# Two KB of scratch for POOL's transfers, the identity in the constants' tile, rooms fixed by name

## The chip, the cores and the metric

One core of one Trainium2 chip. The time is that of one execution on the device, in microseconds (us). The engines are TensorE (PE, its weight loads PEld), VectorE (DVE), ScalarE (ACT), GpSimd (POOL) and SyncE (SP); SP and POOL issue nearly all transfers.

## The reference

Attention over pooled keys and values, then a gated feed-forward network, all in float32:

```python
# q, k, v: (8, 8, 576, 64); keys and values are means over 8 neighbours, so 72 of each
scores = q @ k_p.transpose(0, 1, 3, 2) / 8
attn = exp(scores - max) / (sum + 1e-09)
x = (attn @ v_p).transpose(0, 2, 1, 3).reshape(4608, 512)
out = (sigmoid(x @ w_gate) * (x @ w_val)) @ w_out        # 512 -> 1536 -> 512
```

## The kernel before

The 4608 rows of x are worked on in nine blocks of 512. Block 0 goes first, alone, by a hand-written word list (`ORDER`, carried out by `first_pass`). The other eight go in four rounds of two. A round makes the gate and value products of two blocks as a 2x2 scheme with seven products in place of eight (`product`, tiles `chain`), then the products with `w_out` in the same scheme (`second_sums`, tiles `acc`). Each float32 operand is split in a high and a low part, and each product is made of three products of parts. In between stands the attention of the blocks to come (`attention`), as tasks cut into steps.

Weights are read once as 64-bit words, converted, split, kept in the chip's main memory (`kept...`) and read again in each round: `parts` for gate and value through six rooms, `oparts` for `w_out` through three, issued two units ahead in `second_sums`.

In blocks 4 to 8 the transposes that attention needs are not TensorE's. `turned` has DVE transpose blocks of 32x32 (tile `turn`), then POOL issues 4 to 8 transfers to main memory (tile `turned`) for each call and one back (to `pt` or `pr`). POOL also writes the weights' parts to main memory in round 1 (`reload` with `fresh`). These are the only transfers that POOL issues, and a scratch in the first bytes of each partition serves them: 1024 bytes, an argument of `bacc.Bacc`.

Nothing is issued while the functions run. `Book` takes each call as a numbered unit (a unit can hold several matmuls), and the loop at the end issues the units in the order of the list `LATER`; so the sequence on each engine and queue is fixed by hand. Waits follow from which tile an instruction reads or writes.

Rooms: the pool `rawp` has three rooms in rotation for loads of q, k and v (tile `raw`), `two` has two in rotation for `y` (also `o`) and two for `m`. Rotation gives the next tile a room, and its first writer waits for the readers of the tile before in that room.

Constants: `cst` (128 partitions, 133 words) holds an identity, masks and one number. SP loads it with `nc.sync.dma_start(cst, const)`, as its fifth load. DVE casts the identity to `identr` (type F32R) for the transposes of `r3`. `spare` is a small tile on which POOL's fill and an ACT exponential run at the start.

Of the kernel before, what the change touches and what calls it, by code (L numbers as in the profile page):

```python
# [11 lines left out]
F32 = mybir.dt.float32  # L12
# [7 lines left out]
P = 128  # L20
# [90 lines left out]

LATER = """
# [217 lines left out]
def attention_then_ffn(ctx: ExitStack, tc: tile.TileContext, qT, kT, vm, vr, vn, sums8, wgv, wo, const, out, outT):  # L330
# [34 lines left out]
    def split(h, l, x):  # L365

        nc.scalar.copy(h, x)
        nc.vector.tensor_tensor(out=l, in0=x, in1=h.bitcast(F32), op=ALU.subtract)

    kept = {
        (kind, p, g): dram.tile([P, 2, 2 * HALF], F32R, name=f"kept{kind}{p}{g}")
# [1204 lines left out]
```

## Time and profile before

| | |
|---|---|
| median of 3 runs | 906.82 us (906.38 to 906.93) |
| profiled execution, time | 906.25 us |
| its span, first to last instruction | 904.5 us |
| PE busy | 893.6 us (99%) |
| DVE busy | 657.4 us (73%) |
| ACT busy | 497.1 us (55%) |
| POOL busy | 199.4 us (22%) |
| transfers of POOL's queue (q0) | 15040 packets, 32.79 MB, 10.6% of 16 engines' span |
| transfers of SP's queue (q1) | 85040 packets, 203.84 MB, 66.7% |

The span is the time that the rows below speak of; the execution is 1.75 us longer than it. A matmul's length is modelled and overlaps the next one's, so the mean of one is longer than what it adds. "issue" as the end of an idle time says that nothing in the profile released the instruction. Nearly all rows carry the line 317, which is that of the helper that records calls; the names of the tiles tell them apart.

### The profile page before, as it was taken

How to read it: one execution, taken by the hardware profiler on the slowest of the kernel's cores; microseconds unless marked ns; L12 is line 12 of the kernel's file. 1: busy time of each engine (PE TensorE's matmuls, PEld its weight loads, DVE VectorE, ACT ScalarE, POOL GpSimd, SP SyncE). 2: the span in 40 equal slices, each digit the busy share in tenths (PEclk: the TensorE clock that was granted, in tenths of full speed). 3: DMA queues.
4: the chain of work that ended last, by engine and by line, in shares of the span. 5: the costliest groups of instructions: out<-in, count | busy, mean ns of one | idle time of the engine just before them, and what ended most of it. 6: DMA issues, size and time to landing. Idle time of an engine off the chain costs nothing.

```text
span 904.5 us, 12612 instructions
## 1 busy us (share of the span) xinstructions
PE 893.6 (99%) x4162; PEld 735.1 (81%) x4162; DVE 657.4 (73%) x1039; ACT 497.1 (55%) x1071; POOL 199.4 (22%) x369
## 2 busy tenths in 40 slices
PE   7999999999999999999999999999999999999998
PEld 6788778888888888888888888888888888888886
DVE  7989788889899998757678796356589552224863
ACT  5888887587856475445365554334355542224352
POOL 2412101011164235443343104132213000000000
PEclk9999999999999999999999999999999999999999
DMA  9899888889999888787987787686747775746644
GB/s 342 302 332 349 289 331 303 299 280 330 329 328 313 278 288 287 234 304 260 302 273 245 243 279 260 225 269 198 256 127 249 247 251 201 227 169 205 195 167 141
DMA packets 100289, 237.56 MB, mean 263 GB/s; under 512 B 13856, under 2 KB 34720, under 8 KB 98688
## 3 DMA queue, kind: packets, MB, share of 16 engines
q1 hardware_dynamic: 85040, 203.84, 66.7%
q0 software_dynamic: 15040, 32.79, 10.6%
q8 instruction: 33, 0.54, 0.2%
q14 instruction: 32, 0.26, 0.1%
q10 hardware_dynamic: 144, 0.13, 0.0%
HBM read 176.02 MB, written 60.69 MB: 262 GB/s over the span
## 4 chain that ended last, share of the span: by engine, by line
PE 90%; DVE 4%; DMA 3%; ACT 2%; issue 1%; SPq 0%; DVEq 0%; ACTq 0%
PE chain L317 55%; PE acc L317 27%; PE av L317 4%; PE sc L317 3%; DVE early L317 1%; DMA raw<-in_wgv 1%; DMA raw_o<-in_wo 1%; PE tp L317 1%; DMA raw<-in_vr 1%; DMA h<-in_kT 0%; ACT e L317 0%; DVE s L317 0%; DVE hs L317 0%; DVE h L317 0%; ACT hs L317 0%
## 5 line engine op out<-in xcount | busy, mean ns | idle before, releaser
L317 PE MATMUL chain<-xo,parts 128*128 128x512 f32 x2316 | 543.7, 392 | 0.0
L317 PEld LDWEIGHTS chain<-xo,parts 128*128 128x128 f32 x2316 | 430.7, 188 | 92.5 <-issue 1.0
L317 PE MATMUL acc<-hs,oparts 128*128 128x512 f32 x1008 | 237.3, 391 | 0.3 <-issue 0.2
L317 PEld LDWEIGHTS acc<-hs,oparts 128*128 128x128 f32 x1008 | 188.0, 188 | 40.9 <-issue 1.2
L317 POOL DMA_DIRECT2D turned<-turn x240 | 131.7, 551 | 214.8 <-DVE turn L317 185.2
L317 DVE TENSOR_TENSOR y<-chain,sV 128x512 f32<-128x512 f32 x46 | 31.1, 686 | 69.3 <-PE chain L317 59.0
L317 DVE TENSOR_TENSOR hs<-h,hs 128x1024 fp32r<-128x1024 f32 x52 | 63.0, 1217 | 11.6 <-ACT hs L317 11.4
L317 ACT CAST hs<-h 128x1024 fp32r<-128x1024 f32 x52 | 54.4, 1050 | 30.0 <-PE acc L317 23.1
L317 ACT COPY chain<-chain 128x512 f32<-128x512 f32 x46 | 26.4, 576 | 57.0 <-PE chain L317 47.3
L317 DVE TENSOR_TENSOR y<-chain,sG 128x512 f32<-128x512 f32 x46 | 31.2, 682 | 34.0 <-PE chain L317 23.4
L317 ACT CAST hs<-s 128x1024 fp32r<-128x1024 f32 x36 | 37.5, 1051 | 28.4 <-PE acc L317 13.0
L317 ACT COPY sG<-chain 128x512 f32<-128x512 f32 x46 | 26.7, 586 | 46.5 <-PE chain L317 44.8
L317 DVE TENSOR_TENSOR hs<-s,hs 128x1024 fp32r<-128x1024 f32 x36 | 43.8, 1219 | 11.2 <-ACT hs L317 10.9
L317 ACT COPY sV<-chain 128x512 f32<-128x512 f32 x46 | 26.7, 585 | 38.8 <-PE chain L317 36.1
L317 DVE SCALAR_TENSOR_TENSOR h<-gate,chain 128x512 f32<-128x512 f32 x46 | 30.6, 677 | 21.8 <-PE chain L317 21.7
L317 ACT ACTIVATE gate<-chain 128x512 f32<-128x512 f32 x46 | 26.9, 594 | 34.2 <-PE chain L317 31.7
L317 PE MATMUL sc<-kbd,raw 128*128 128x144 f32 (+1 forms) x262 | 41.2, 296 | 0.1
L317 PEld LDWEIGHTS sc<-kbd,raw 128*128 128x128 f32 (+1 forms) x262 | 33.6, 176 | 7.9 <-issue 2.8
L317 ACT ACTIVATE gate<-y 128x512 f32<-128x512 f32 x46 | 28.9, 633 | 19.1 <-DVE y L317 19.0
L317 PE MATMUL acc<-oparts,hs 128*128 128x512 f32 x144 | 38.7, 402 | 0.2 <-ACT oparts L317 0.2
L317 DVE TENSOR_REDUCE m<-sc 128x4 f32<-128x288 f32 x48 | 21.7, 452 | 18.2 <-PE sc L317 17.7
L317 DVE SCALAR_TENSOR_TENSOR h<-gate,y 128x512 f32<-128x512 f32 x46 | 31.0, 683 | 0.3
(211 smaller groups left out, 1073.8 us busy)
## 6 DMA issues: line engine op xcount, KB each, us to landing
oparts<-keptS SPq DMA_DIRECT2D x48, 512.0 KB, 4.4
oparts<-keptO SPq DMA_DIRECT2D x72, 256.0 KB, 4.2
raw<-in_wgv SPq DMA_DIRECT2D x12, 1024.0 KB, 8.5
out<-o SPq DMA_DIRECT2D x35, 256.0 KB, 3.6
raw<-in_kT SPq DMA_DIRECT2D x28, 288.0 KB, 5.0
raw<-in_qT SPq DMA_DIRECT2D x29, 256.0 KB, 4.7
raw<-in_vm SPq DMA_DIRECT2D x24, 256.0 KB, 5.6
raw_o<-in_wo SPq DMA_DIRECT2D x12, 512.0 KB, 8.1
```

The lines of the kernel that those rows point to most:

```text
L317: return self._book.take(lambda: f(*args, **named))
```

## The change

Six edits:

- The scratch is 2048 bytes.
- `cst` is a tile of type F32R, 136 words; `cst` and `identr` are two views of it. The tile `identr` and DVE's cast are gone.
- The load of the constants is POOL's, with both sides as F32R.
- `spare` takes its room from the tag `rz`.
- The three rotating pools become one-room pools with tags that carry a number; strings (`RAWS`, `YS`, `MS`) give the number for each tile in the order in which the tiles are asked for.
- `LATER` is written anew for one unit less.

```diff
+RAWS = (
+    "21012001220111021201020120200212010202122010021021020121012010110021011220110"
+)
...
-6 5 4 7 0 11 3 2 21 8 25 27 19 28 14 18 23 31 22 20 9 26 13 35 17 36 33 1 10 40 45 76 39 37 12 48 47 52 16 55 32 66 38
...
-    cpool, work, two = sb("cpool"), sb("work"), sb("two", 2)
-    rawp, wpool, opool = sb("rawp", 3), sb("wpool"), sb("opool")
+    cpool, work, two = sb("cpool"), sb("work"), sb("two")
+    rawp, wpool, opool = sb("rawp"), sb("wpool"), sb("opool")
...
-    cst = cpool.tile([P, P + 16], F32, name="cst")[:, :P + 5]
+    constr = cpool.tile([P, P + 8], F32R, name="cst")[:, :P + 5]
+    cst, identr = constr.bitcast(F32), constr[:, :P]
...
-    identr = cpool.tile([P, P], F32R, name="identr")
-    spare = cpool.tile([P, 8], F32, name="spare")
+    spare = work.tile([P, LINE], F32, name="spare", tag="rz")[:, :8]
...
+    raws, ys, ms = iter(RAWS), iter(YS), iter(MS)
+
+    def raw_tile():
+        return rawp.tile([P, S], F32, name="raw", tag=f"raw{next(raws)}")
+
+    def y_tile(name):
+        return two.tile([P, BT], F32, name=name, tag=f"y{next(ys)}")
+
+    def m_tile():
+        return two.tile([P, LINE], F32, name="m", tag=f"m{next(ms)}")
...
-        return fill(rawp.tile([P, S], F32, name="raw"), *what)
+        return fill(raw_tile(), *what)
...
-        gate = two.tile([P, BT], F32, name="y", tag="y")
+        gate = y_tile("y")
...
-    nc.sync.dma_start(cst, const)
-    nc.vector.tensor_copy(identr, ident)
+    nc.gpsimd.dma_start(constr, const.bitcast(F32R))
...
-    nc = bacc.Bacc("TRN2", target_bir_lowering=False, num_devices=1, dynamic_dma_scratch_size=1024)
+    nc = bacc.Bacc("TRN2", target_bir_lowering=False, num_devices=1, dynamic_dma_scratch_size=2048)
```

## Rows read from the trace of the kernel before

**Rows 1.** Windows: length, busy us of PE, PEld, DVE, ACT, POOL, clock, transfers' share, GB/s.

```profile
0.00:28.00 28.00, 23.32 (x120) 18.38 (x121) 22.08 (x50) 17.09 (x38) 8.27 (x27) 1.00 0.94 343
28.00:248.00 220.00, 218.24 (x1073) 179.31 (x1072) 193.60 (x350) 175.38 (x480) 35.38 (x60) 1.00 0.89 313
248.00:707.00 459.00, 458.89 (x2128) 379.51 (x2127) 346.61 (x533) 232.12 (x449) 155.48 (x283) 1.00 0.80 261
707.00:904.50 197.50, 193.13 (x847) 157.94 (x845) 95.15 (x108) 72.53 (x107) 0.26 (x1) 1.00 0.58 198
```

**Rows 2.** TensorE's waits, whole span: who waited for whom, us, times, longest.

```profile
PE idle L317 <- POOL kbd L318: 1.7, 1, 1.7
...
PE tp L317 <- ACT y L317: 0.7, 1, 0.7
...
PE av L317 <- DVE pl L317: 0.5, 1, 0.5
...
PE vr L317 <- DMA xs<-in_vn: 0.2, 1, 0.2
```

**Rows 3.** TensorE's waits after 248 us.

```profile
PE acc L317 <- issue: 0.2, 1, 0.2
```

**Rows 4.** The chain that ended last, first 32 us: start, us, what.

```profile
2.12 4.28 DMA h<-in_kT
...
7.54 0.13 DVE identr L317
...
20.43 0.62 PE tp L317 x4
```

**Rows 5.** Timeline of the start: start, us, engine, line, operation, tiles, shape, count, idle.

```profile
2.59 0.43 SPq L317 DMA_DIRECT2D cst<-in_const  x1
2.96 0.20 POOL L318 MEMSET vfull<- 128x128 f32 x1
...
6.42 0.75 DVE L317 TENSOR_REDUCE early<-h 128x72 f32<-128x576 f32 x1 [1.19 <-DMA h<-in_kT]
...
16.04 1.04 POOL L317 TENSOR_SCALAR w<-w 128x1024 f32<-128x1024 f32 x1 [12.87 <-ACT w L317]
```

**Rows 6.** The page's costliest groups, two of TensorE.

```profile
L317 PE MATMUL chain<-xo,parts 128*128 128x512 f32 x2316 | 543.7, 392 | 0.0
...
L317 PE MATMUL acc<-hs,oparts 128*128 128x512 f32 x1008 | 237.3, 391 | 0.3 <-issue 0.2
```

**Rows 7.** The tile cst: first reader (ns, first and last start); its load's landing.

```profile
L317 PE MATMUL tp<-cst,early x36: 270/273/328, 14.7 to 146.6; 128*128 128x128 f32 x36
...
DMA to landing us min/median/max: 4.0/4.0/4.0
```

**Rows 8.** The tiles turned: who waited for their transfers (us, times); landing.

```profile
  POOL pt L317: 12.8, 3
...
  DVE turn L317: 5.0, 3
...
DMA to landing us min/median/max: 1.7/3.9/7.1
```

**Rows 9.** POOL's timeline, one burst.

```profile
276.24 3.95 POOL L317 DMA_DIRECT2D turned<-turn  x7 [3.43 <-DVE turn L317]
281.51 0.55 POOL L317 DMA_DIRECT2D turned<-turn  x1 [1.31 <-issue]
```

**Rows 10.** That burst's first transfer alone.

```profile
DMA to landing us min/median/max: 5.0/5.0/5.0
```

**Rows 11.** POOL's waits that end without a releaser, ahead of turned.

```profile
POOL turned L317 <- issue: 12.2, 13, 2.6
```

**Rows 12.** POOL's timeline, another burst.

```profile
247.43 0.53 POOL L317 DMA_DIRECT2D keptG2C<-parts  x1 [0.27 <-DVE vrc L317]
...
254.99 1.12 POOL L317 DMA_DIRECT2D turned<-turn  x2 [1.91 <-DMA keptG2C<-parts]
```

**Rows 13.** The page's transfers: count, KB each, median us to landing.

```profile
oparts<-keptS SPq DMA_DIRECT2D x48, 512.0 KB, 4.4
```

More of the change, by code (lines that the diff above doesn't have):

```diff
@@ L109 @@
 """
-LATER = """
[155 rows of a table removed]
+RAWS = (
+    "21012001220111021201020120200212010202122010021021020121012010110021011220110"
+)
+YS = (
+    "1001010110100110101010100001100100110101101010101010010110010101010110100110101001011000111010100110"
+    "10101001100101011011000110010101"
+)
+MS = (
+    "010101010101010101010101010101010101010101010101"
+)
+LATER = """
[150 rows of a table added]
 """
@@ L741, in attention @@
                 scv = sc.rearrange("p i (h k) -> p (i h) k", h=2)
-                m = two.tile([P, LINE], F32, name="m")[:, :QT]
+                m = m_tile()[:, :QT]
                 nc.vector.reduce_max(out=m, in_=scv, axis=AX.X, negate=j in BIASED)
@@ L896, in product @@
         if m in (3, 7):
-            y = two.tile([P, BT], F32, name="y", tag="y")
+            y = y_tile("y")
             nc.vector.tensor_tensor(out=y, in0=t, in1=seen[kind, {3: 6, 7: 5}[m]], op=ALU.add)
@@ L1077, in result @@
             else:
-                t = two.tile([P, BT], F32, name="o", tag="y")
+                t = y_tile("o")
             r, a = (half * 2 + c) * P, (2 * n - 2 + side) * BT
@@ L1202, in first_pass @@
         rooms = narrow + [space(BT)] + [wide[i // 2][:, i % 2] for i in range(4)]
-        rooms += [rawp.tile([P, S], F32, name="raw") for _ in range(3)]
+        rooms += [raw_tile() for _ in range(3)]
         scs, rests, av, vp, raws, conv, ygate, vbank, hss, acc, outs, turned = ({} for _ in range(12))
@@ L1450, in gate @@
         def gate(f):
-            ygate[f] = two.tile([P, BT], F32, name="y", tag="y")
+            ygate[f] = y_tile("y")
             nc.scalar.activation(ygate[f], vbank[0, f], AF.Tanh)
```

304 rows, old and new, of the table LATER are left out of this document.

## The prediction

> **What bounds the kernel now.** I read the stretches first. From 28 us to 707 us TensorE is busy for 218.24 + 458.89 = 677.13 of 679 us, at a granted clock of 1.00; in the middle stretch, the only one in which POOL moves the turned tiles, it is idle for 459.00 - 458.89 = 0.11 us [rows 1]. The reader is to see that no other engine comes near that: DVE is busy for 346.61 of those 459 us, POOL for 155.48. Then TensorE's waits: the longest is 1.7 us, nearly all end on a compute engine, and the one that ends on a transfer is 0.2 us long [rows 2]. After 248 us a single wait is left, 0.2 us, and nobody released it [rows 3]. So a gain can come from three places: the first 28 us, where TensorE is busy for 23.32; the 220 - 218.24 = 1.76 us lost between 28 and 248 us; and the last 197.5 us, where 4.37 us are lost [rows 1] and nothing of this change is at work any more.
>
> The start is set by DVE, not by TensorE. In the chain of waits the third load of keys is issued at 2.12 us and takes 4.28 us; from 6.42 us the chain runs through DVE, with the cast of the identity in it for 0.13 us (7.54 to 7.67), until the transposes at 20.43 us, and no load ends a step of it in between [rows 4]. DVE's row says the same: it stood idle for 1.19 us before 6.42 us, for that load [rows 5].
>
> **The change part by part.**
>
> *The order.* The new list is the old one without number 1 (the cast), every later number lowered by one; all 3,799 entries agree. So each engine keeps its instructions in the same sequence, but for the cast, which goes from DVE, and the load of the constants, which goes from SP to POOL.
>
> *Named rooms.* The strings give each of the 77 raw, 132 y and 48 m tiles the room that the rotating pools gave it before, by the addresses of the tiles in that program. Same room, same earlier reader, same wait: 0. The floor and the ceiling of this are both nothing, since no wait changes.
>
> *Addresses.* The scratch grows by 1,024 bytes in each partition; the identity's 512, the spare tile's 32 and 32 of the constants' go. Everything behind moves by 448 bytes. What an address is worth no row shows by itself; the nearest are TensorE's own: products whose operands lie in different pools take 392 and 391 ns each [rows 6]. One ns on the 237.3/1008 = 0.235 us that such a matmul occupies, over 3,324 of them, would be 3.3 us either way. I take 0, the row's own difference being a pipelined length and not a spacing.
>
> *The spare tile* now lies in the room of rz, used first at block 3, after the exponential on it at 2 us is long over: 0.
>
> *The cast goes.* It stands in the chain for 0.13 us, a part of its own length only, since DVE's instructions overlap there [rows 4]. What is late next is DVE's own next instruction, so the whole 0.13 us reaches the transposes at 20.43 us: -0.13. The identity's rounded form is needed only after the first transposes on the constants [rows 7] and lands with them.
>
> *The constants on POOL.* SP loses one issue, of 0.43 us [rows 5]. The loads behind it go out that much earlier, into transfers that are busy for 0.94 of this stretch [rows 1], and the chain rests on none of them [rows 4]: 0. POOL has ended its fills at 2.96 + 0.20 = 3.16 us, does nothing until 16.04 us and waits there for ACT [rows 5], so behind the load nobody waits on POOL; SP's loads keep their own queue. The first reader of the constants is the transposes' at 14.7 us [rows 7]. From 3.16 us that leaves 11.5 us; the longest landing of any of POOL's 270 transfers to and from turned tiles was 7.1 us, the median 3.9 [rows 8]. So the load is hidden with 4.4 us to spare. If that cover is gone, each us past 14.7 is one us of TensorE's.
>
> What the load takes from the others: on SP it landed 4.0 us after 2.59 us, at 6.6 us, and the keys before it at 2.12 + 4.28 = 6.40 us [rows 4, 7], so it occupies the transfers for about 0.2 us. Behind the keys, as before, that costs DVE nothing; ahead of them it delays 6.42 us by 0.2 us. Bounds: 0 to +0.2. I take 0, because POOL can begin it only 3.16 - 2.12 = 1.04 us after SP has issued the keys.
>
> The Trainium skill, "DMA: Bandwidth & Descriptors", section "Queues, rings and completion order", speaks against that choice: each DMA engine goes round between the queues that have work, packet by packet, so a load on a queue of its own does not stand behind SP's line. By it the sum would be -0.13 + 0.2; no row here has the two queues side by side at the start. It is the second rival below.
>
> *The scratch.* In before, POOL issues seven transfers of a burst back to back, then stands idle for 1.31 us ahead of the eighth, released by nothing that the profile shows [rows 9]; the first of the seven lands 5.0 us after 276.24 us, at 281.24 [rows 10], and the eighth starts at 281.51. So the eighth waits for the first to land: I read that as a full scratch. Idle time of this sort is 12.2 us in 13 places ahead of the turned tiles [rows 11]. Bounds of what twice the room takes from POOL: 0 to 12 us. Of that the end of the kernel gets what reaches TensorE. Who waits for these transfers: POOL itself for 12.8 us ahead of pt, DVE for 5.0 [rows 8], TensorE never [rows 2, 3]. The cover is the distance between a tile's turning and its use; the ceiling is TensorE's idle time in that stretch, 0.11 us [rows 1]. I take 0, with -0.1 and the loss of the fourth rival as ends.
>
> **The sum.** -0.13 (cast) + 0 + 0 + 0 = -0.13 us. The profiled execution took 906.25 us, 1.75 around a span of 904.5; with the change 906.12. The median of the runs shown, 906.82, lies 0.57 above that execution, so the time is 906.7 us. A measurement of this kernel can tell about 0.2% from no change, 1.8 us; the sum is a fourteenth of that.
>
> **Rivals.**
>
> 1. *The scratch gives POOL nothing or little.* There is a second limit: at 254.99 us POOL had waited 1.91 us for the landing of keptG2C, the eighth transfer before [rows 12]. If eight may be out at once in any case, twice the scratch buys the step from seven to eight. POOL's idle rows then stay in part; the time is the same 906.7. I give it 0.12 as the case in which most of the 12.2 us stay.
>
> 2. *The constants go ahead of the keys* (the rule above): -0.13 + 0.2, 906.9. For it: POOL is free at 3.16 us, while the keys are still landing until 6.40. Chance 0.12.
>
> 3. *Faster.* The shifted start lets the stalls of 28 to 248 us close: -0.13 - 1.76 - 0.11 = -2.0, 904.8. Against it: those waits end on ACT and DVE (y, pl) [rows 2], whose work is unchanged, and start with them. It would take nearly all of them to pass 1.8 us. Chance 0.13, in which I count also a gain by the addresses.
>
> 4. *Slower: the reloads of the second products come late.* With the scratch no longer holding POOL back, the eighth and later transfers of a burst run beside SP's reloads of oparts. These land in 4.4 us [rows 13] and are issued two units ahead, 24 products of 0.235 us = 5.6 us [rows 6]; the lead is 1.2 us at the median. One more transfer of 48 KB at the stretch's 261 GB/s [rows 1] takes 0.19 us of it. From the point at which a reload has less lead than that, TensorE pays; if 15 of the 63 reloads between 248 and 707 us do, 15 x 0.19 = 2.9 us, 909.6. For it: the lead is small and the transfers are busy 0.80 of the stretch. Against: 0.11 us of idle TensorE says that none is late now, and the bytes are the same, only some 1.3 us earlier. Chance 0.11.
>
> 5. *The constants land too late.* If POOL's load stood behind SP's line and landed with the transfers of 16 us, the transposes at 14.7 us would start 1.3 us late: 908.0. Against it the 4.4 us to spare. Chance 0.04.
>
> **How the numbers follow.** The forecast itself has 0.48. It, rivals 1 and 2 lie within 0.2% of 906.82 (905.0 to 908.6): 0.48 + 0.12 + 0.12 = 0.72 for no difference. Rival 3: 0.13 for faster. Rivals 4 and 5: 0.15 for slower, the last to the edge only. The likeliest case's own range is 906.1 to 907.3, what three runs scatter. The range asked for reaches to where rival 3 would about end and part of the way to rival 4: 905.0 to 908.8.
>
> **What would show it.** The cast gone from DVE's rows and the chain's first transposes at 20.3 us: the cast's term right; at 20.5 us: rival 2. A landing of the constants before 14.7 us, and no wait of TensorE on them: the load is hidden. No idle time without a releaser ahead of an eighth transfer: the scratch did it; the same idle time now ended by the landing of an earlier transfer: rival 1. TensorE's waits after 248 us still under 0.5 us: the relief reached nobody. Waits of acc on oparts' transfers would show rival 4; they, or a longer matmul at the same clock, would make this prediction wrong.

## The result, and the profile after

The changed kernel took 919.91 us (median of 4 runs, 919.63 to 920.94), beside 906.79 us (906.38 to 906.93) for the kernel before on the same chip: a ratio of 1.0148, 95% interval 1.0130 to 1.0165. The forecast was 906.7 us, the end of its range 908.8. The kernel became 1.5% slower; none of the named rivals gives that.

The profiled execution's span is 918.2 us, against 904.5. First the stretches of the changed kernel, with the columns of [rows 1] (length, busy us of PE, PEld, DVE, ACT, POOL, PE's granted clock, the transfers' share, GB/s):

```profile
0.00:28.00 28.00, 23.95 (x117) 19.17 (x118) 22.25 (x49) 16.56 (x36) 8.30 (x28) 1.00 0.94 343
28.00:248.00 220.00, 219.03 (x1069) 179.05 (x1068) 192.20 (x348) 174.62 (x477) 34.45 (x58) 1.00 0.88 312
248.00:707.00 459.00, 459.00 (x2094) 374.47 (x2093) 344.34 (x532) 228.23 (x445) 153.34 (x281) 1.00 0.79 257
707.00:918.20 211.20, 206.82 (x888) 166.14 (x886) 99.81 (x112) 77.70 (x114) 2.45 (x5) 1.00 0.60 197
```

The reader is to see what is *not* there. TensorE has not become idle: its busy times add up to 908.80 us, so it is idle for 9.4 us of 918.2, where before it was for 10.9 (904.5 less the 893.58 of [rows 1]). The clock is 1.00 in every row. What fell is the number of matmuls in equal time: in the middle stretch 2,094 where [rows 1] has 2,128, with TensorE busy throughout in both. Each one takes longer. The last stretch is longer since the work that did not fit before 707 us is done there.

Which ones, the page's groups say. Of the changed kernel, the three large groups of matmuls with 128x512 moving elements (busy us, mean ns | idle before them):

```profile
L323 PE MATMUL chain<-xo,parts 128*128 128x512 f32 x2316 | 554.5, 396 | 0.6 <-ACT xs L323 0.6
...
L323 PE MATMUL acc<-hs,oparts 128*128 128x512 f32 x1008 | 241.7, 396 | 0.1
...
L323 PE MATMUL acc<-oparts,hs 128*128 128x512 f32 x144 | 38.6, 402 | 0.0
```

And of the kernel before, the third of these (the other two are [rows 6]):

```profile
L317 PE MATMUL acc<-oparts,hs 128*128 128x512 f32 x144 | 38.7, 402 | 0.2 <-ACT oparts L317 0.2
```

Against [rows 6], `chain` gains 554.5 - 543.7 = 10.8 us and `acc` on `hs` 241.7 - 237.3 = 4.4 us: 15.2 us together. That is all of TensorE's growth (908.8 - 893.6 = 15.2); with the 1.5 us less of idle time it gives the 13.7 us of the span. The third group, the 144 products of block 0 with `w_out`, has the same shape and gained nothing.

The length of one matmul is modelled and overlaps the next, so I worked out the **spacing** from the trace: the time from the start of one such matmul to the start of the next, where both belong to the same group (some 2,190 pairs in `chain`). Its median is 227 ns before (eight in ten from 226 to 231) and 232 ns after (229 to 240), alike in the three stretches after 28 us; for the 144 products of block 0 it is 227 ns in both. Sixty such products in a row show it with hardly any model in it, since only the end of the last one is modelled. TensorE's timeline (start, busy us), before and then after:

```profile
402.41 13.88 PE L317 MATMUL chain<-xo,parts 128*128 128x512 f32 x60
```

```profile
406.08 14.19 PE L323 MATMUL chain<-xo,parts 128*128 128x512 f32 x60
```

0.31 us over 60 is 5 ns for each.

What is different about them is where their operands lie. In before, the rooms of the moving rows (`xo`, `hs`, in the pool `work`) and of the weights (`parts`, `oparts`, in `wpool` and `opool`) both start at 32 modulo 512 bytes of a partition. In the changed kernel the moving rows start at 96 and the weights at 480. `spare` now asks for the tag `rz` before any other tile of `work` does, so that room of 128 bytes comes first in the pool and pushes the rooms that lay ahead of it, those of `xo` and `hs` among them, 448 + 128 = 576 bytes on. Everything behind the pool, which only holds the same rooms in another order, moves by 448. The **distance**, weights less moving rows modulo 256 bytes, went from 0 to 128. The 144 products of block 0 with `w_out` have both operands in `work`: their distance stayed 0.

### The profile page after: what moved, and what is told of

It reads as the page before. It is cut to its first block, busy times and chain, and to the rows that moved or that the text cites. A ratio compares the mean times of both kernels' runs of the same rounds, so it can differ in the third digit from the quotient of the medians.

```text
span 918.2 us, 12611 instructions
## 1 busy us (share of the span) xinstructions
PE 908.8 (99%) x4162; PEld 738.8 (80%) x4162; DVE 658.6 (72%) x1038; ACT 497.1 (54%) x1071; POOL 198.6 (22%) x370
## 4 chain that ended last, share of the span: by engine, by line
PE 95%; DVE 2%; DMA 1%; ACT 1%; issue 0%; SPq 0%; DVEq 0%; ACTq 0%
PE chain L323 58%; PE acc L323 28%; PE sc L323 4%; PE av L323 4%; DVE early L323 1%; DMA raw<-in_wgv 1%; PE tp L323 1%; DMA h<-in_qT 0%; ACT early L323 0%; DVE w L323 0%; DVE parts L323 0%; DVE h L323 0%; ACT raw L323 0%; DVE oparts L323 0%; PE tr L323 0%
## 5 line engine op out<-in xcount | busy, mean ns | idle before, releaser
L323 PE MATMUL chain<-xo,parts 128*128 128x512 f32 x2316 | 554.5, 396 | 0.6 <-ACT xs L323 0.6
L323 PE MATMUL acc<-hs,oparts 128*128 128x512 f32 x1008 | 241.7, 396 | 0.1
```

What stands on the lines that cost most here:

```text
L323: return self._book.take(lambda: f(*args, **named))
```

## The experiments

Theory R: the distance between the moving rows and the weights sets the spacing. It was first written down modulo 512 bytes; the modulo of 256 came out of the runs with 256 and 64 bytes below. Rivals: S, the larger scratch (or POOL's faster transfers); W, the place of the weights alone; N, the place of other rooms or the order of the pools.

**`spare` in another room of the same pool.** All of the change is kept but this line. `ph` is a room of `work` that then comes first, and its size keeps the distance at 0.

```diff
-    spare = work.tile([P, LINE], F32, name="spare", tag="rz")[:, :8]
+    spare = work.tile([P, BT], F32, name="spare", tag="ph")[:, :8]
```

> The changed kernel with one line different: the spare tile takes its room from ph (2048 bytes) and not from rz (128 bytes). Twice the scratch, POOL's load of the constants and the shared identity stay. The rooms of work then start 480 bytes past a multiple of 512, as the weights' rooms do, so a product's moving rows and its weights again lie a multiple of 512 bytes apart, as in the kernel before; in the changed kernel they lie 128 bytes off that. Theory R (the distance between the two operands, modulo 512 bytes, sets the spacing of the products): spacing back from 232 to 227 ns, time 906 to 907.5 us. Theory S (the wider scratch or POOL's load slows TensorE): about 920 us. Theory W (the weights' own start, 32 bytes past a multiple of 512 before and 480 after, sets it): about 920 us.

Measured: 906.55 us (905.80 to 908.26, 10 runs), beside 906.75 for before: 0.9998 (0.9988 to 1.0008). All of the loss is gone, with the scratch at 2048 bytes. Its page:

```profile
L323 PE MATMUL chain<-xo,parts 128*128 128x512 f32 x2316 | 543.9, 392 | 0.7 <-ACT xs L323 0.7
L323 PE MATMUL acc<-hs,oparts 128*128 128x512 f32 x1008 | 237.0, 391 | 0.2 <-issue 0.2
```

**`spare` alone.** The kernel before, with only the room of `spare` moved; the scratch is still 1024 bytes.

```diff
-    spare = cpool.tile([P, 8], F32, name="spare")
+    spare = work.tile([P, LINE], F32, name="spare", tag="rz")[:, :8]
```

> The kernel before with one edit of the change alone: the spare tile takes its room from rz. The scratch is 1024 bytes, SP loads the constants, the cast and the identity's own tile stay. rz's room of 128 bytes thereby becomes the first of work, and the moving rows lie 128 bytes off the weights modulo 512, as in the changed kernel. Theory R: spacing 232 ns, 919 to 921 us. Theory S: 906.8 us, no difference. Theory W: the weights start at a multiple of 512; if only their own start counts, 906 to 908 us would be likely, since no line is crossed.

Measured: 920.44 us (920.09 to 921.18), ratio 1.0155 (1.0140 to 1.0170): this one line makes the whole loss, and S falls.

```profile
L317 PE MATMUL chain<-xo,parts 128*128 128x512 f32 x2316 | 554.5, 396 | 0.0
L317 PE MATMUL acc<-hs,oparts 128*128 128x512 f32 x1008 | 241.7, 396 | 0.1
```

**A gap between the two pools, nothing else.** The kernel before, with unused bytes behind `work`; the pool `two` holds two of each tile, so 32 words are 256 bytes, 24 are 192, 8 are 64. First 256 and 64:

```diff
     cpool, work, two = sb("cpool"), sb("work"), sb("two", 2)
+    two.tile([P, 32], F32, name="gap")
```

> The kernel before with an unused 256 bytes between the rooms of work and those behind them, nothing else: moving rows stay 32 bytes past a multiple of 512, weights go from 32 to 288. Theory R: not 227 ns; a distance of 256 is the farthest from 0, so the spacing is 232 ns or more and the time 920 us or more. Theory S: 906.8 us. Theory W: any value, since this start was not seen yet.

> The kernel before with an unused 64 bytes between the rooms of work and those behind them: weights start 96 bytes past a multiple of 512, moving rows 32. Theory R: a distance of 64 bytes; if any distance other than 0 costs, 910 to 920 us; if only that of 128 does, 906.8. Theory S: 906.8 us. Theory W: 906.8 us, since in the changed kernel weights that start at 96 (the products of block 0 with w_out) kept a spacing of 227 ns.

One run of each: 904.97 us with 256 bytes (spacing 227 ns), 921.33 us with 64 (233 ns). The rooms behind moved four times as far in the first, and nothing came of it. R as written down, modulo 512, had expected 232 ns or more and 920 us or more there, and missed; from here on R is read modulo 256, at least for this step. The page of the kernel with 64:

```profile
L317 PE MATMUL chain<-xo,parts 128*128 128x512 f32 x2316 | 556.0, 397 | 0.0
```

**The same 128 bytes on either side of the weights.** In the first kernel only the rooms behind the weights (`h`, `snap`) move; in the second the weights move too.

```diff
     hpool, snap = sb("hpool"), sb("snap")
+    hpool.tile([P, 32], F32, name="gap")
```

> The kernel before with an unused 128 bytes behind the weights' rooms: only the tiles h and those of snap move by 128 bytes, which VectorE and ScalarE read and write; moving rows and weights both stay 32 bytes past a multiple of 512. Theory R (the distance between a product's two operands): spacing 227 ns, 905 to 908 us. Theory N (any room that moves against the rooms of work costs, through the other engines' traffic): 232 ns, about 920 us.

```diff
-    rawp, wpool, opool = sb("rawp", 3), sb("wpool"), sb("opool")
+    rawp, gap, wpool, opool = sb("rawp", 3), sb("gap"), sb("wpool"), sb("opool")
+    gap.tile([P, 32], F32, name="gap")
```

> The kernel before with an unused 128 bytes directly ahead of the weights' rooms, so that weights, h and snap move by 128 bytes and raw, y, m and the moving rows stay. It differs from the kernel with 128 bytes behind the weights (904.3 us) in the place of the weights' rooms alone. Theory R (the distance from moving rows to weights, modulo 256): 232 ns, 919 to 921 us. Theory N (some other room against the rooms of work): 227 ns, 904 to 907 us.

One run of each: 904.32 and 921.71 us (the second in another session, its kernel before at 908.00). TensorE's groups, first kernel, then second:

```profile
L317 PE MATMUL chain<-xo,parts 128*128 128x512 f32 x2316 | 543.6, 392 | 0.0
```

```profile
L317 PE MATMUL chain<-xo,parts 128*128 128x512 f32 x2316 | 554.8, 396 | 0.1
```

The two differ by the place of the weights alone. The second kernel's granted clock was low at its start, 0.82 in the mean of the first 28 us (for a part of them it was at its lower level, 1.2 GHz), which cost a part of its time; in its later stretches it was 1.00 (columns as in [rows 1]), and the row of 60 products in the middle takes 14.25 us there, 13.91 in the first kernel. So N falls. The transfers that fill the weights' rooms moved with them; that these slow TensorE is not excluded by a run of its own, but in the changed kernel the spacing is 232 ns alike in the stretches in which the transfers are busy for 0.88, 0.79 and 0.60.

```profile
0.00:28.00 28.00, 24.02 (x110) 20.00 (x111) 20.49 (x48) 15.49 (x36) 5.98 (x26) 0.82 0.92 331
...
248.00:707.00 459.00, 459.00 (x2093) 374.22 (x2092) 343.98 (x535) 229.06 (x449) 152.89 (x278) 1.00 0.78 257
```

W falls as well: in the changed kernel and in the one with `spare` in `ph` the weights start at the same 480 modulo 512, and the spacing is 232 ns in one and 227 in the other. The modulo of 256 also gets a second witness here: modulo 512 the distance is 128 in the kernel with the gap ahead of the weights and 384 in the changed kernel, and the spacing is 232 ns in both.

**Other distances.** 32 bytes by a pool of its own, 192 by the pool `two` as above, 224 by a pool of its own as well:

```diff
     cpool, work, two = sb("cpool"), sb("work"), sb("two", 2)
+    sb("gap").tile([P, 8], F32, name="gap")
```

> The kernel before with an unused 32 bytes between the rooms of y and m and those behind them: weights start 64 bytes past a multiple of 512, moving rows 32; a distance of 32 bytes, the smallest that rooms can have. If the cost falls off from 0 as the distance grows (64: 233 ns, 128: 232), 32 costs at least as much, 233 ns or more and 921 us or more; if a short distance is as good as none, 227 ns and 907 us.

```diff
     cpool, work, two = sb("cpool"), sb("work"), sb("two", 2)
+    two.tile([P, 24], F32, name="gap")
```

> The kernel before with an unused 192 bytes between the rooms of work and those behind them: weights start at 224, moving rows at 32. If only the distance modulo 256 counts (0 and 256 gave 227 ns, 64 and 128 gave 233 and 232), 192 is a slow one: 232 to 233 ns, 919 to 922 us. If the cost falls off toward 256: between 227 and 232 ns, 910 to 916 us.

```diff
     cpool, work, two = sb("cpool"), sb("work"), sb("two", 2)
+    sb("gap").tile([P, 56], F32, name="gap")
```

> The kernel before with an unused 224 bytes ahead of raw's and the weights' rooms: weights start 224 bytes past the moving rows, modulo 256. The spacing was 227 ns at 0 and 256, 233 at 32 and 64, 232 at 128 and 229 at 192. If the cost falls steadily toward 256: 228 ns, 907 to 909 us. If it is a step that ends at 192: 227 ns, 904 to 907 us. If any distance but 0 costs like the small ones: 233 ns, 920 us.

One run of each: 920.83 us with 32 bytes, 911.39 with 192, 922.86 with 224. That they are slow is R. How slow, no single shape that I had written down says: 192 fits a cost that falls off toward 256, and 224 fits a cost that is the same for any distance but 0. The distance of 192 costs a third of the others; 224, though nearer to 256, costs as much as 32 and 64: beside the kernel before of their sessions the three lose 14.4 to 14.9 us, and runs of one and the same kernel lie further apart than that. The page of the kernel with 192, where the values of the spacing lie in clusters at 226, 229 and 232 ns:

```profile
L317 PE MATMUL chain<-xo,parts 128*128 128x512 f32 x2316 | 548.2, 394 | 0.4 <-ACT xs L317 0.4
```

**The change with the distance at 0 and the pools in another order.** The kernel of the first experiment, with the weights ahead of `rawp`, so that their distance is 256 modulo 512.

```diff
-    rawp, wpool, opool = sb("rawp"), sb("wpool"), sb("opool")
+    wpool, opool, rawp = sb("wpool"), sb("opool"), sb("rawp")
```

> The changed kernel with the spare tile in the room of ph, and the pool of raw tiles placed behind the weights' pools and no longer ahead of them: the distance of moving rows and weights becomes 256 bytes modulo 512, and no byte is added. If 256 is as good as 0: the time of the kernel with the spare in ph, 906.5 us, and a ratio of 0.999 to 1.001 to the kernel before. If 256 is better than 0 (one look at the kernel before with it gave 904.97 us): 904.5 to 905.5 us, ratio 0.998. If the wider scratch costs something that the first look hid: above 908 us.

Measured: 906.26 us (904.71 to 908.04, 11 runs) beside 906.42: 0.9993 (0.9981 to 1.0005), spacing 227 ns. Modulo 256 holds, and there is nothing to gain from the order. No kernel tried is shown to be faster than the kernel before. The single runs of 904.32 and 904.97 us lie 0.2 and 0.1 us below the lowest of its own runs in their sessions (904.54 to 909.84 and 905.11 to 908.61), which one run each can't tell from chance; with eleven runs, the distance of 256 gains nothing.

## Why the prediction was wrong, step by step

**The step that failed** is *Addresses*, "Everything behind moves by 448 bytes", and the 0 that was put on it, with *The spare tile* "0" beside it. The first is false in a way that the diff shows: a tag's room lies where the tag is first asked for, so giving `spare` the tag `rz` put that room at the front of `work`. I asked of the spare tile only who reads its room, not where the room goes. So the pools did not shift as one; `work` went 128 bytes further. The price was bounded too narrowly as well. The bound in the text, 1 ns on 3,324 products, is 3.3 us; measured were 10.8 + 4.4 = 15.2 us, or 15.2/3,324 = 4.6 ns each. The row it was taken from compared 392 with 391 ns, two groups which both have a distance of 0, so it could not show what a distance costs. The kernel with `spare` in `ph` is the change as the prediction described it, with both pools in step: 906.55 us, where 906.7 was forecast.

**TensorE bounds, and a longer matmul is paid in full**: right, and the last sentence of the prediction named "a longer matmul at the same clock" as what would make it wrong.

**The order, named rooms**: 0, as the kernel with `spare` in `ph` bears out with all the rest in one sum (0.9998). Alone they were not tried.

**The cast goes, -0.13 us**: not seen. The first transposes of the chain started at 21.06 us, not at the 20.3 of the forecast or the 20.43 of [rows 4]. What holds the start in this execution is the load of the queries, as the chain of waits of the changed kernel shows (start, us, what):

```profile
1.66 4.30 DMA h<-in_qT
6.10 4.19 PE sc L323 x16
...
21.06 0.62 PE tp L323 x4
```

That is neither the missing cast nor the moved load of the constants: the kernel before with `spare` alone, which keeps the cast and SP's load, has the same chain (load 4.35 us, transposes at 21.10), and among the kernels made from before by a gap the landing of the keys takes from 4.25 to 5.29 us. The start scatters by more than the term; a sum to 0.13 us had no meaning there.

**The constants on POOL: hidden**: right. The tile `cst` in the changed kernel (first reader; the load; its landing):

```profile
L323 PE MATMUL tp<-cst,early x36: 270/273/330, 15.3 to 147.6; 128*128 128x128 f32 x36
...
L323 POOL DMA_DIRECT2D cst<-in_const x1: 717/717/717, 3.1 to 3.1; - x1
...
DMA to landing us min/median/max: 5.5/5.5/5.5
```

It landed at 3.1 + 5.5 = 8.6 us, 6.7 us ahead of the reader, so rival 5 is out. Rival 2 (the constants ahead of the keys) can't be told apart in that scatter: the slowest keys, 5.29 us, are in a kernel whose constants SP loads.

**The scratch: POOL is freed, TensorE gets nothing**: right. POOL's waits ahead of `turned` that nothing in the profile ends (us, times, longest):

```profile
POOL turned L323 <- issue: 1.6, 8, 0.3
```

It was 12.2 us in 13 [rows 11]. The burst of [rows 9, 10], in the changed kernel:

```profile
278.15 3.90 POOL L323 DMA_DIRECT2D turned<-turn  x7 [3.60 <-DVE turn L323]
282.26 0.55 POOL L323 DMA_DIRECT2D turned<-turn  x1 [0.21 <-issue]
285.46 0.56 POOL L323 DMA_DIRECT2D pt<-turned  x1 [2.64 <-DMA turned<-turn]
```

The stop of 1.31 us ahead of the eighth transfer is 0.21. Rival 1 is there in part: some transfers now wait for an earlier one to land, as the 1.91 us of [rows 12] did before:

```profile
375.39 0.55 POOL L323 DMA_DIRECT2D turned<-turn  x1 [0.73 <-DMA pt<-turned]
376.86 2.18 POOL L323 DMA_DIRECT2D turned<-turn  x4 [0.92 <-DMA turned<-turn]
```

Waits of this sort ahead of `turned`, on landings of earlier transfers to `turned`, grew from 6.3 us in 8 places to 9.6 in 10, so a part of the relief was turned into them. Idle time without a releaser also grew ahead of `pt`, from 5.8 us in 6 places to 11.3 in 3; what ends it is not shown. In time it is the same: the kernel with `spare` in `ph` has as little of the idle time ahead of `turned` (1.3 us left) and is no faster.

**Rivals 3 and 4.** Faster: between 28 and 248 us TensorE's idle time did fall, from 1.76 to 0.97 us, beside work that had become longer; with the distance at 0 no gain can be measured. Late reloads of `oparts`: TensorE's waits show none, in any stretch. (The 63 reloads which that rival counts between 248 and 707 us are not what the trace has: 85 transfers to `oparts` are issued there. Nothing hung on it.) The slower time came from none of the waits that the rivals dealt with.

## What to carry to other kernels

When a change moves a room, write down the new address of every operand of the bounding engine, not only who reads the room; a tile that asks first for a tag shifts a whole pool. Where one engine is busy for 99%, compare busy times by group before looking for waits: here equal counts, an equal clock and a longer mean pointed to the operands. In this kernel, keep moving rows and weights at a distance of 0 modulo 256 bytes; against 32, 64, 128 or 224 that was worth 13 to 15 us, against 192 some 5.

## What the runs showed of the hardware

That the distance of two operands in a partition matters to TensorE was new to me. For the 128x512 products in `chain`, here is the spacing over the whole execution, nearly all of it at a granted clock of 1.00 (2.4 GHz):

| distance mod 256 | spacing, median ns | busy `chain`, us | time, us | kernels |
|---|---|---|---|---|
| 0 | 227 | 543.6 to 544.0 | 904.3 to 906.8 | before, 256, behind, `ph`, order |
| 32 | 233 | 555.8 | 920.83 | one run |
| 64 | 233 | 556.0 | 921.33 | one run |
| 128 | 232 | 554.5 to 554.8 | 919.9 to 921.7 | after, `spare` alone, gap |
| 192 | 229 | 548.2 | 911.39 | one run |
| 224 | 234 | 555.9 | 922.86 | one run |

The median hides a rhythm. Within a long row of `chain` products at some 380 us the spacings repeat: 227, 227, 226 ns at a distance of 0; 231 and 236 in turn at 64; 226, 229, 232 at 192; 231, 235, 233, 234 at 224. At 128 it is a cycle of seven in the changed kernel (240, 233, 231, 231, 229, 230, 232), and 229 and 238 in turn in the kernel with the gap ahead of the weights. So the cost is not a fixed one for each product.

The dependence is shown for long rows of 128x512 products only. The attention's products `av` on `ph`, `pl` and `pr`, most of them narrower and mixed with others, went from a distance of 0 to 128 by the same move of `spare`, since their weights lie in `cpool`. Their four groups are busy for 55.2 us before and 55.3 after.

The Trainium skill, "SBUF — State Buffer", section "Who interferes with whom", says that TensorE has two read ports, one for the moving operand and one for weight loads, independent of each other. That lets one expect nothing of the distance; here it is worth 5 ns on 227, and the measurement decides. Why the distance counts stays open: no run took the weight loads away, and nothing here explains why 192 is cheap and 224 is not. What is shown is the dependence.
